# The opening of batch 0 by row tile in order of landing, x of batch 2 ahead of all second weights, and batch 1 turned behind the second axis

## The chip, the cores and the metric

The kernel runs on one core of one Trainium2 chip. The metric is the device time of one execution in microseconds, as the median of several executions. The profile of one execution gives a *span*, from the first to the last counted instruction; it is about 2 us shorter than the timed figure. The *granted clock* is the share of TensorE's full clock that the profile shows as granted to it (1.00 is all of it). On one core a single run has no second core to be compared with, so the state of a run (fast or slow) is read against the fastest run of the same kernel. Only fast runs are compared here, except where the text says otherwise.

## The reference

Eight batches pass an attention between `x` (512 rows per head) and a small `state` (32 rows per head), then a two-dimensional Fourier transform of which the real part is kept, a normalization and two dense layers.

```python
B, H, S, Ns, D = (8, 8, 512, 32, 64)
def _attn_ref(x, state):
    scores = scale * x @ state^T            # softmax over the 32 state rows
    xread  = softmax(scores) @ state        # 512 rows
    sread  = softmax(scale * state @ x^T) @ x   # 32 "state rows"
    return concatenate([xread, sread], axis=2)  # 544 rows, d_model = 512
def _moe_ref(x, w_ch1, w_ch2):
    mixed = real(fft(fft(x, axis=1), axis=2))
    u  = x + mixed
    un = (u - mean(u)) / sqrt(var(u) + 1e-6)
    return u + maximum(un @ w_ch1, 0) @ w_ch2   # 512 -> 2048 -> 512
```

(Shortened.) The kernel does the transforms as matmuls with cosine and sine tables: the *first axis* runs over the rows (products `gp`), the *second axis* over the 512 columns (products `yp`). Rows are first folded into even and odd parts (`Sm`, `SS`), so that half the products suffice. Layer 1 is `ph`, layer 2 is `po`.

## The kernel before

All engines are scheduled by hand: each executes its instructions in the order in which the program lists them. TensorE (PE) streams the two layers of all batches almost without a gap. The argument is about the first 60 us, in which batch 0 has nothing to hide behind. The parts that matter are these. First, the clears of buffers of the attention, which stand on GpSimd behind the request of the first weights; then the later loads:

```python
def clears(i):
    nc.gpsimd.memset(XFs[i][:, :, 512:514], 0.0)
    # ... (borders of XR, XO, XOl, and all of XN, XQl)

nc.gpsimd.tensor_copy(gate, xs_of[0][:, 0:2048:512])      # wait for all of x of batch 0
for q in range(4):
    nc.gpsimd.dma_start(out=w1[:, :, q * 512:(q + 1) * 512], in_=w1v[:, :, q * 512:(q + 1) * 512])
more_constants()
clears(0)

def more_loads():
    state_blocks(1, 2, nc.gpsimd.tensor_copy)
    nc.gpsimd.tensor_copy(gate[:, 0:1], XQ0[:, 3, 0, 0:1])
    cast_x(1)
    nc.gpsimd.tensor_tensor(gate, xs_of[0][:, 0:4], w1[:, :, 3 * 512], op=ALU.add)
    turn_in_dram(3, B)
    load_x(2)
    # ...
def last_loads():
    nc.gpsimd.tensor_copy(gate[:, 0:1], xs_of[2][:, 0:1])  # one row tile of x of batch 2
    for q in range(4):
        nc.gpsimd.dma_start(out=w2[:, q * 4:(q + 1) * 4, :], in_=w2v[:, q * 4:(q + 1) * 4, :])
    state_blocks(2, 3, nc.gpsimd.tensor_copy)
```

A "gate" is a tiny GpSimd operation that reads what it is to wait for; since GpSimd works in order, everything listed behind it waits too. Second, the order of the first part, in which `t0` are the steps of batch 0's transform, `s1` and `r1` scores and reads of batch 1, `L` and `M` layer-1 and layer-2 blocks, and `turns1` PE's transposes of x of batch 1:

```python
for step in (warmed(t0[:2], 2) + [alternate, more_loads] + warmed(t0[2:4], 2) + [exp_again, last_loads,
        t0[4], t0[8], W(6), turns1, t0[5], W(10), t0[7], copies1[0], copies1[1], t0[6], copies1[2],
        L[0], s1[0], t0[9], L[1], t0[10], s1[1], L[2], t0[11], t0[12], L[3], s1[2], r1[0], L[4], s1[3],
        r1[2], lambda: (cast_x(2), turned[2](), load_x3()), t0[13], L[5], r1[1], L[6], r1[3], L[7], r1[4], r1[5], L[8], r1[7],
        lambda: state_ones(2, B), lambda: [r() for r in first_roots], L[9], L[10]]):
    step()
```

Third, the row sum of a batch, a VectorE operation with two bf16 inputs in SBUF (the on-chip buffer), which recurs in every batch:

```python
def fold_rows(k, eng=nc.vector):
    eng.tensor_add(Sm[:, k], XF[:, k], XR[:, k])
```

The softmax here doesn't subtract the row's maximum and nothing guards it: scores larger than these inputs give would overflow.

Of the kernel before, what the change touches and what calls it, by code (L numbers as in the profile page):

```python
# [12 lines left out]
F32 = mybir.dt.float32  # L13
BF16 = mybir.dt.bfloat16
# [16 lines left out]
def kernel(  # L31
# [26 lines left out]
    psX = ctx.enter_context(tc.tile_pool(name="psX", bufs=1, space=bass.MemoryType.PSUM))  # L58
    psQ = ctx.enter_context(tc.tile_pool(name="psQ", bufs=3, space=bass.MemoryType.PSUM))
    psF = ctx.enter_context(tc.tile_pool(name="psF", bufs=3, space=bass.MemoryType.PSUM))  # L60
# [8 lines left out]
    mhalfpi = singles.tile([128, 1], F32, name="mhalfpi")  # L69
    pi_ = singles.tile([128, 5], I32, name="pi_")  # L70
# [4 lines left out]
    ltq = lt.rearrange("p (q i) -> p q i", q=2)  # L75
    nc.gpsimd.iota(ltq[:, :, 0:64], pattern=[[1, 2], [2, 64]], base=1, channel_multiplier=0)
# [3 lines left out]
    nc.gpsimd.iota(pi_[:, 0:2], pattern=[[128, 2]], base=1, channel_multiplier=1)  # L80
    nc.gpsimd.iota(pi_[:, 3:4], pattern=[[0, 1]], base=0, channel_multiplier=1)
    nc.gpsimd.iota(pi_[:, 4:5], pattern=[[0, 1]], base=128, channel_multiplier=-1)
    for hh in range(4):
        nc.gpsimd.iota(pi_[32 * hh:32 * hh + 32, 2:3], pattern=[[0, 1]], base=129, channel_multiplier=1)
    nc.gpsimd.iota(li[:, 0:128], pattern=[[2, 128]], base=1, channel_multiplier=0)
    nc.gpsimd.iota(li[:, 128:256], pattern=[[2, 128]], base=2, channel_multiplier=0)
    nc.gpsimd.iota(li[:, 256:384], pattern=[[2, 128]], base=1, channel_multiplier=0)
    make_identity(nc, ident)
    mirror = singles.tile([128, 128], BF16, name="mirror")
    halves = ((halfpi, PI / 2), (mhalfpi, -PI / 2), (epst, eps), (mhalf, -0.5))  # L90
    sg = singles.tile([128, 5], F32, name="sg")
    sgi = singles.tile([128, 1], I32, name="sgi")

    def more_constants():
        for t, v in halves:
            nc.gpsimd.memset(t, v)
        nc.gpsimd.memset(mirror, 0.0)
        nc.gpsimd.affine_select(out=mirror, in_=mirror, compare_op=ALU.not_equal, fill=1.0, base=-127,
                                pattern=[[1, 128]], channel_multiplier=1)
# [13 lines left out]
    def load_x(b):  # L113
        xs = wk.tile([128, 4 * dm], F32, name="xs", tag="xs")
        xs_of[b] = xs
        v = xs.rearrange("p (i h d) -> p i h d", i=4, d=D)
        xb = x[b].rearrange("h s d -> s h d")
        for ps, si, rows in (
            (slice(0, 128), 0, xb[1:129]),
            (slice(0, 128), 1, xb[144:272]),  # L120
            (slice(0, 128), 2, xb[273:401]),
            (slice(32, 128), 3, xb[416:512]),
            (slice(0, 15), 3, xb[129:144]),
            (slice(16, 31), 3, xb[401:416]),
            (slice(15, 16), 3, xb[0:1]),
            (slice(31, 32), 3, xb[272:273]),
        ):
            queue = nc.scalar if b == 0 and si in (0, 2) else nc.sync
            queue.dma_start(out=v[ps, si], in_=rows)  # L129
# [4 lines left out]
    load_state(0, 1)  # L134
    load_x(0)
    load_state(1, 2)
    load_x(1)
# [5 lines left out]

    turn_in_dram(2, 3)
    load_state(2, 3, s_dram)
# [24 lines left out]
    state_blocks(0, 1)  # L170
    cast_x(0, nc.scalar.copy, 0, 1)
    cast_x(0, nc.scalar.copy, 1, 2)
    cast_x(0, lo=2, hi=3)
    cast_x(0, lo=3, hi=4)
# [16 lines left out]
    XQ0 = XQs[0].rearrange("p (j k c) -> p j k c", j=4, k=2)  # L191
# [5 lines left out]
    TN = singles.tile([128, NM], BF16, name="TN")  # L197
    TE = singles.tile([128, 512], BF16, name="TE")
    TO = singles.tile([128, 512], BF16, name="TO")

    pf = singles.tile([128, 5], F32, name="pf")
# [5 lines left out]
    def turn(W, N, lf, cols, scratch):  # L207
        n = len(cols)
        f2d, q2d = scratch[:, 0:n * W], scratch[:, n * W:2 * n * W]
        f, q = [t.rearrange("p (n w) -> p n w", w=W) for t in (f2d, q2d)]  # L210
        for i, c in enumerate(cols):
            nc.vector.tensor_scalar(q[:, i, :], in0=lf, scalar1=pn[:, c:c + 1], scalar2=float(1 << 23), op0=ALU.mult, op1=ALU.add)
        nc.vector.tensor_scalar(q2d, in0=q2d, scalar1=float(1 << 23), scalar2=-float(N), op0=ALU.subtract, op1=ALU.mult)
        for i, c in enumerate(cols):
            nc.vector.scalar_tensor_tensor(f[:, i, :], in0=lf, scalar=pf[:, c:c + 1], in1=q[:, i, :], op0=ALU.mult, op1=ALU.add)
        absolute(q2d, f2d)
        return f, q
# [12 lines left out]
    f1, q1 = turn(NM, Stot, lt, [0, 2], gen1)  # L230

    fi = gen2[:, 0:384].bitcast(I32)
    f2 = gen2[:, 384:768]
    q2_ = gen2[:, 2048:2432]
    nc.vector.tensor_scalar(fi[:, 0:256], in0=li[:, 0:256], scalar1=pf[:, 3:4], scalar2=None, op0=ALU.mult)
    nc.vector.tensor_scalar(fi[:, 256:384], in0=li[:, 256:384], scalar1=pf[:, 4:5], scalar2=None, op0=ALU.mult)
    turn_w = 2.0 * PI / dm * shrink


    def second_table():  # L240
        nc.vector.tensor_scalar(fi, in0=fi, scalar1=dm - 1, scalar2=None, op0=ALU.bitwise_and)
        nc.vector.tensor_scalar(f2, in0=fi, scalar1=float(dm // 2), scalar2=None, op0=ALU.subtract)
        absolute(q2_, f2)
        nc.vector.tensor_scalar(sgi, in0=pi_[:, 3:4], scalar1=1, scalar2=None, op0=ALU.bitwise_and)
        nc.vector.tensor_scalar(sg[:, 0:1], in0=sgi, scalar1=-2.0, scalar2=1.0, op0=ALU.mult, op1=ALU.add)
        nc.vector.tensor_scalar(sg[:, 2:3], in0=sg[:, 0:1], scalar1=-PI / 2, scalar2=None, op0=ALU.mult)
        nc.vector.tensor_scalar(sg[:, 3:4], in0=sg[:, 0:1], scalar1=turn_w, scalar2=None, op0=ALU.mult)





    def sines():
        w = 2.0 * PI / Stot * shrink
        nc.scalar.activation(TC, q1, AF.Sin, bias=halfpi, scale=-w)
        nc.scalar.activation(TS, f1, AF.Sin, bias=0.0, scale=w)
        nc.scalar.activation(TS[32:64, 1, :], q1[32:64, 1, :], AF.Sin, bias=halfpi[32:64], scale=-w)
# [4 lines left out]
    def more_sines():  # L262
        w = 2.0 * PI / dm * shrink
        te, to = [t.rearrange("p (a h c) -> p a h c", a=2, h=2) for t in (TE, TO)]
        q, f = [t.rearrange("p (a c) -> p a c", c=128) for t in (q2_, f2)]
        nc.scalar.activation(te[:, :, 0], q[:, 0:2], AF.Sin, bias=mhalfpi, scale=w)
        nc.scalar.activation(te[:, :, 1], q[:, 0:2], AF.Sin, bias=sg[:, 2:3], scale=sg[:, 3:4])
        nc.scalar.activation(to[:, :, 0], f[:, 2:0:-1], AF.Sin, bias=0.0, scale=w)
        nc.scalar.activation(to[:, :, 1], f[:, 2:0:-1], AF.Sin, bias=0.0, scale=sg[:, 3:4])
# [3 lines left out]

    def alternate():
        for lo, v in ((0, 0.5), (256, 1.0)):
            nc.gpsimd.memset(TO[0:1, lo:lo + 256:2], -v)
            nc.gpsimd.memset(TO[0:1, lo + 1:lo + 256:2], v)

# [11 lines left out]
    nc.gpsimd.tensor_copy(gate, xs_of[0][:, 0:2048:512])  # L290
    for q in range(4):
        nc.gpsimd.dma_start(out=w1[:, :, q * 512:(q + 1) * 512], in_=w1v[:, :, q * 512:(q + 1) * 512])
    more_constants()
    clears(0)

    def more_loads():
        state_blocks(1, 2, nc.gpsimd.tensor_copy)
        nc.gpsimd.tensor_copy(gate[:, 0:1], XQ0[:, 3, 0, 0:1])
        cast_x(1)
# [590 lines left out]
```

## Time and profile before

| | before |
|---|---|
| median of 4 runs in this comparison | 304.88 us (304.45 to 305.28) |
| span of the profiled run, mean granted clock | 302.7 us, 1.00 |
| second axis of batch 0 begins (first `yp`) | 23.21 us |
| layer 1 begins (first `ph` on `unT`) | 27.71 us |
| rest, from there to the end | 275.0 us |
| second weights asked for; landed by quarter | 29.55; 36.4 to 46.2 us |

The lines of the page and of PE's timeline stand in the prediction below. Two more views of the kernel before are needed. The first is VectorE's timeline; a line reads start, duration, engine, source line, operation, output<-inputs, sizes, count, and in brackets the idle time just before with what ended it.

```profile
12.22 0.69 DVE L449 TENSOR_TENSOR XR<-xrp,rs 128x512 bf16<-128x512 f32 x1 [0.40 <-POOL XR L281]
...
42.44 0.43 DVE L507 TENSOR_TENSOR Sm<-XF,XR 128x514 bf16<-128x514 bf16 x1
```

The first line is the first read multiply of batch 0: it waited 0.40 us for GpSimd (POOL) to clear the border of its output `XR`, at 12.2 us. So short a wait is easily passed over; it will matter that the clear came at 12.2 and not how long it was waited for. The second is the row sum of batch 1, unhindered: 0.43 us.

The second view is the queue of SyncE, which issues most transfers (SPq).

```profile
25.15 6.33 SPq L129 DMA_DIRECT2D xs<-in_x_dram  x8
34.02 2.59 SPq L360 DMA_TRANSPOSE sT<-stb  x2
```

x of batch 2 is asked for from 25.15 us on, before the two DMA transposes of its state.

### The profile page before, as it was taken

The page shows a single profiled execution, that of the slowest core. Times are in us where ns is not written, and L with a number is a line of the kernel's source. Part 1 is how long each engine was busy: PE and PEld are TensorE (multiplying, and loading weights), DVE is VectorE, ACT ScalarE, POOL GpSimd, SP SyncE. Part 2 cuts the span into 40 slices and gives each one's busy share as a digit, 9 for nine tenths or more (in the row PEclk, how much of TensorE's full clock was granted, in tenths as well). Part 3 has the DMA queues.
Part 4 walks back from the last instruction along what each step waited for, and adds up shares of the span by engine and source line. Part 5 has one row for each costly group of instructions (what it writes and reads, how often), then busy time and mean ns, then how long its engine had stood idle before and what let it go on. Part 6 is the DMA issues. An engine that isn't in the chain of part 4 may idle for free.

```text
span 302.7 us, 6048 instructions
## 1 busy us (share of the span) xinstructions
PE 290.6 (96%) x2326; PEld 166.7 (55%) x2326; DVE 179.5 (59%) x433; ACT 139.5 (46%) x267; POOL 96.6 (32%) x217
## 2 busy tenths in 40 slices
PE   5868999999999999999999999999999999999996
PEld 4756997545544555456544555445454544555443
DVE  7696784867888395754727575675668474000012
ACT  6777865746633553254533445254524442334200
POOL 4987784490271034400315022702240131000000
PEclk9999999999999999999999999999999999999999
DMA  7997999144733943467242765253333023600355
GB/s 160 210 200 171 182 174 220 50 89 110 171 87 72 208 122 89 105 137 170 68 116 70 151 146 106 69 123 70 87 89 69 37 69 87 138 2 35 71 135 142
DMA packets 110906, 34.86 MB, mean 115 GB/s; under 512 B 102062, under 2 KB 106414, under 8 KB 110878
## 3 DMA queue, kind: packets, MB, share of 16 engines
q1 hardware_dynamic: 100158, 28.72, 42.3%
q0 software_dynamic: 4224, 4.19, 8.6%
q10 hardware_dynamic: 6496, 1.57, 2.3%
q8 instruction: 18, 0.29, 0.4%
q14 instruction: 10, 0.08, 0.1%
HBM read 22.41 MB, written 14.02 MB: 120 GB/s over the span
## 4 chain that ended last, share of the span: by engine, by line
PE 87%; DVE 3%; POOL 3%; ACT 3%; SPq 1%; DMA 1%; issue 1%; POOLq 0%; DVEq 0%; ACTq 0%
PE po L793 36%; PE ph L729 34%; PE ph L739 4%; PE gp L610 3%; PE po L785 1%; SPq L129 1%; PE xrp L440 1%; PE xfp L440 1%; PE yp L565 1%; PE yp L564 1%; PE esp L415 1%; PE eTp L427 1%; POOL xin L132 1%; DMA xs<-in_x_dram 1%; DVE U L569 1%; ACT XR L470 1%
## 5 line engine op out<-in xcount | busy, mean ns | idle before, releaser
L793 PE MATMUL po<-w,hT 128*128 128x512 bf16 x496 | 124.2, 379 | 0.0
L731 ACT ACTIVATE hT<-ph 128x512 bf16<-128x512 f32 x112 | 66.8, 597 | 118.2 <-PE ph L729 116.1
L729 PE MATMUL ph<-unT,w 128*128 128x512 bf16 x448 | 113.8, 379 | 0.0
L729 PEld LDWEIGHTS <-w 128*128 128x128 bf16 x576 | 50.7, 98 | 47.0
L793 PEld LDWEIGHTS <-hT 128*128 128x128 bf16 x496 | 46.9, 98 | 46.5
L760 DVE SCALAR_TENSOR_TENSOR ot<-po,rstd,U 128x512 f32<-128x512 f32 (+2 forms) x33 | 24.2, 733 | 51.1 <-PE po L793 48.9
L614 POOL COPY GL<-G 128x128 bf16<-128x128 bf16 x8 | 2.3, 291 | 75.4 <-ACT G L611 75.4
L569 DVE TENSOR_TENSOR U<-yp,XR 128x512 f32<-128x512 f32 x16 | 10.9, 683 | 26.0 <-PE yp L565 26.0
L326 POOL TENSOR_TENSOR rstd<-mv,epst 128x1 f32<-128x1 f32 x34 | 7.5, 221 | 47.3 <-DVE mv L322 47.3
L327 POOL TENSOR_TENSOR rstd<-rstd,mhalf 128x1 f32<-128x1 f32 x34 | 21.2, 624 | 2.7
L320 DVE BATCH_NORM_STATS2 st<-U 128x6 f32<-128x512 f32 x32 | 21.8, 682 | 0.1
L611 ACT CAST G<-gp 128x288 bf16<-128x288 f32 x31 | 14.6, 485 | 7.6 <-PE gp L610 7.6
L739 PE MATMUL ph<-unT,w 128*128 128x128 bf16 x256 | 16.1, 219 | 0.5 <-ACT unT L650 0.5
L132 POOL CAST xin<-xs 128x2048 bf16<-128x2048 f32 (+1 forms) x9 | 14.5, 1616 | 3.6 <-DMA xs<-in_x_dram 3.3
L813 PE MATMUL warm<-ident 128*128 128x128 bf16 x144 | 12.0, 232 | 3.7 <-POOL ident masks.py:199 3.6
L739 PEld LDWEIGHTS <-w 128*128 128x128 bf16 x256 | 15.0, 98 | 0.8 <-issue 0.6
L638 DVE TENSOR_SCALAR ub<-U,mv 128x512 bf16<-128x512 f32 x24 | 12.3, 513 | 0.9
L491 POOL COPY XT<-XR 32x514 bf16<-32x514 bf16 x8 | 4.8, 603 | 23.4 <-DVE XR L449 23.1
L813 PEld LDWEIGHTS <-ident 128*128 128x128 bf16 x144 | 9.9, 104 | 4.1 <-POOL ident masks.py:199 3.6
L449 DVE TENSOR_TENSOR XR<-xrp,rs 128x512 bf16<-128x512 f32 x16 | 11.1, 695 | 1.0 <-POOL XR L281 0.4
L741 ACT ACTIVATE hT<-ph 128x512 bf16<-128x512 f32 x16 | 9.3, 597 | 3.2 <-PE ph L739 3.1
L569 DVE TENSOR_TENSOR U<-yp,XF 128x510 f32<-128x510 f32 x16 | 10.8, 674 | 0.0
(187 smaller groups left out, 367.1 us busy)
## 6 DMA issues: line engine op xcount, KB each, us to landing
xs<-in_x_dram SPq DMA_DIRECT2D x22, 256.0 KB, 4.5
w<-in_moe_w_ch_dram POOLq DMA_DIRECT2D x8, 512.0 KB, 10.9
out_dram<-ot SPq DMA_DIRECT2D x15, 256.0 KB, 3.1
r_dram<-ot SPq DMA_DIRECT2D x14, 256.0 KB
out_dram<-r_dram SPq DMA_DIRECT2D x14, 256.0 KB, 3.5
xs<-in_x_dram SPq DMA_DIRECT2D x8, 192.0 KB, 3.4
xs<-in_x_dram ACTq DMA_DIRECT2D x2, 256.0 KB
l_dram<-ot SPq DMA_DIRECT2D x2, 256.0 KB
```

Source lines behind the costliest of these rows:

```text
L132: copy(xin_bufs[b % 2][:, lo:hi, 1:513], xs_of[b].rearrange("p (i c) -> p i c", i=4)[:, lo:hi])
L320: nc.vector.bn_stats(st6, u)
L327: nc.gpsimd.tensor_tensor(rstd, rstd, mhalf, op=ALU.pow)
L569: nc.vector.tensor_add(u.rearrange("p (k r) -> p k r", r=2), p.rearrange("p (r k) -> p k r", r=2)[:, 0:u.shape[1] // 2, :], x.rearrange("p ...
L611: (nc.vector.tensor_copy if b == 0 and j == 3 else nc.scalar.copy)(G[:, j, :].rearrange("p (i q) -> p q i", q=2), p[:, 0:NM].rearrange("p ...
L638: nc.vector.tensor_scalar(t, in0=ud, scalar1=mv[:, 0:1], scalar2=None, op0=ALU.subtract)
L729: nc.tensor.matmul(ph[:, o:o + n], lhsT=w1[:, c, f * 128:(f + 1) * 128], rhs=un_of[key][:, c, :], start=(c == 0), stop=(c == DC - 1))
L731: nc.scalar.activation(hT[:, per * i:per * i + per, :].rearrange("p a b -> p (a b)"), ph, AF.Relu, scale=-1.0 if key in flipped else 1.0)
L739: nc.tensor.matmul(ph[:, o:o + 128], lhsT=w1[:, c, f * 128:(f + 1) * 128], rhs=un_of[key][:, c, 128 * r:128 * r + 128], start=(c == 0), st ...
L760: nc.vector.scalar_tensor_tensor(ot[:, cols], in0=po_of[i][:, 0:cols.stop - cols.start], scalar=rstd, in1=u[:, cols], op0=ALU.mult, op1=AL ...
L793: nc.tensor.matmul(po_of[i], lhsT=h_of[key][:, f, i * 128:(i + 1) * 128], rhs=w2[:, f, :], start=(f == 0), stop=(f == FC - 1))
L813: nc.tensor.matmul(t[:, 0:128], lhsT=ident, rhs=ident, start=(i == 0), stop=(i == n - 1))
```

## The change

The intent has three parts. (1) Batch 0 passes its opening one row tile at a time, in the order in which the tiles of x land (2, 0, 3, 1): transpose, score, one exponential, read. The state rows go through four matmuls where eight small copies were; half of the second-axis tables are computed by a multiply on VectorE instead of two more sines; statistics and roots of batch 0 are put off. (2) All of x of batch 2 is to be there before the second weights are asked for. (3) PE transposes batch 1 behind both second-axis products, not between them. The core of the diff, with cuts marked:

```diff
@@ loads of x @@
+        if b == 0:
+            for queue, n in ((nc.sync, None), (nc.scalar, 2), (nc.sync, 3), (nc.scalar, 0), (nc.sync, 4), (nc.sync, 5), (nc.sync, 6),
+                             (nc.sync, 1)):
# ...
@@ half tables @@
+    def second_halves():
+        nc.vector.tensor_scalar(TEO[:, :, 1], in0=TEO[:, :, 0], scalar1=sg, scalar2=None, op0=ALU.mult)
+        nc.vector.tensor_scalar(TEO[0:1, 2], in0=TEO[0:1, 2], scalar1=0.5, scalar2=None, op0=ALU.mult)
# ...
@@ GpSimd's early work @@
-    nc.gpsimd.tensor_copy(gate, xs_of[0][:, 0:2048:512])
# ...
+    for i in (3, 1):
+        cast_x(0, lo=i, hi=i + 1)
     for q in range(4):
         nc.gpsimd.dma_start(out=w1[:, :, q * 512:(q + 1) * 512], in_=w1v[:, :, q * 512:(q + 1) * 512])
-    more_constants()
+    constants()
     clears(0)
# ...
-    def last_loads():
-        nc.gpsimd.tensor_copy(gate[:, 0:1], xs_of[2][:, 0:1])
+    def load_w2():
+        nc.gpsimd.tensor_copy(gate, xs_of[2][:, 0:2048:512])
         for q in range(4):
             nc.gpsimd.dma_start(out=w2[:, q * 4:(q + 1) * 4, :], in_=w2v[:, q * 4:(q + 1) * 4, :])
-        state_blocks(2, 3, nc.gpsimd.tensor_copy)
# ...
@@ order, after the opening @@
+    over_d(0)
+    add_sums(0, 1)
+    centre_sums(0, 1)
+    over_d(1)
+    turns1()
+    keep_low()
+    clear_state(2, 3)
+    state_blocks(2, 3, nc.gpsimd.tensor_copy)
+    turned[2, 0]()
+    make_mirror()
+    nc.gpsimd.tensor_tensor(gate, xs_of[0][:, 0:4], w1[:, :, 3 * 512], op=ALU.add)
+    load_x(2)
# ...
+    L[6]()
+    r1[2]()
+    load_w2()
+    r1[1]()
+    L[7]()
+    r1[3]()
+    L[8]()
+    r1[4]()
+    cast_x(2)
+    turned[2]()
+    load_state(3, B, s_dram)
+    load_x(3)
# ...
```

## The prediction

> **What bounds the kernel now.** I read the page first: engine totals, then the slices.
>
> ```profile
> span 302.7 us, 6048 instructions
> ...
> PE 290.6 (96%) x2326; PEld 166.7 (55%) x2326; DVE 179.5 (59%) x433; ACT 139.5 (46%) x267; POOL 96.6 (32%) x217
> ...
> PE   5868999999999999999999999999999999999996
> ...
> PEclk9999999999999999999999999999999999999999
> ```
>
> TensorE (PE) is the bound, at full clock, but only from the fifth slice on (7.6 us each). What can be won lies in the first four, and busy there does not mean useful: much of it is "warm" matmuls on an identity. So next I read PE's timeline for the first real matmul of layer 1 (line L739).
>
> ```profile
> 23.21 0.27 PE L564 MATMUL yp<-TE,G 128*128 128x256 bf16 x1
> ...
> 24.40 0.50 PE L813 MATMUL warm<-ident 128*128 128x128 bf16 x6
> 25.18 1.07 PE L387 MATMUL xTp<-ident,xin 128*128 128x128 bf16 x16 [0.28 <-POOL xin L132]
> ...
> 26.30 0.72 PE L813 MATMUL warm<-ident 128*128 128x128 bf16 x10
> ...
> 27.71 1.22 PE L739 MATMUL ph<-unT,w 128*128 128x128 bf16 x16 [0.46 <-ACT unT L650]
> ```
>
> Columns: start, duration, what, count, idle before. Layer 1 starts at 27.71; 302.7 - 27.71 = 275.0 us follow. Comparing each later matmul's start-to-start time with its shape's median, I find only 4.75 us of excess in those 275: 0.63 before the scores of batch 1 (28.7), 0.30 twice near 40, 1.3 from 56 to 64, the rest in pieces of about 0.1 that return every batch. The tail after the last matmul is 3.2. So the time is the start of layer 1, plus about 270 us of fixed streaming, plus stalls.
>
> The chain of waits tells why the start is 27.71 (start, duration, what):
>
> ```profile
> 4.95 2.52 DMA xs<-in_x_dram
> 7.52 0.63 POOL xin L132
> ...
> 10.53 0.60 ACT ET L406
> 11.13 0.98 ACT E L420 x2
> 12.12 0.92 ACT L260
> ...
> 16.25 1.17 POOL Sm L507
> ...
> 23.22 1.91 POOL xin L132
> ...
> 25.18 1.07 PE xTp L387 x16
> ```
>
> All four row tiles wait for the last piece of x (7.47 us); then all exponentials, the sine table load, eight small copies of the state rows (13.62 to 16.18), the fold on GpSimd, and last GpSimd's cast of batch 1, which PE must transpose before it reaches batch 0's own transpose.
>
> **What the Trainium skill says.** "TensorE: Matmul & The Clock Gate", Wait — 56ns, not 53.3ns?: warm start-to-start 55.6 ns at 128 columns, 215.7 at 512. The trace agrees: medians 56 and 216. "ScalarE: Activation LUTs", What ACT_TABLE_LOAD costs: about 1283 ns per load. The trace has 1.28 us at each of three; the change keeps three. "SBUF — State Buffer", Who interferes with whom: a VectorE (DVE) operation with two SBUF inputs excludes a GpSimd operation that reads SBUF, and the later waits. The trace fits: the fold of 514 columns took 0.93 us at 16.76 beside GpSimd's own fold, 0.43 at 42.44. "DMA: Bandwidth & Descriptors", Anatomy of one DMA: about 2 us fixed. The 64 KB state load took 2.74 (0.73 to 3.47).
>
> **The change, part by part.** The order of instructions shows that after the first layer-1 matmul both kernels have the same 4109 PE rows, in the same numbers by shape. So nothing is gained in the stream itself. I walk the new opening with durations of the old trace.
>
> *Loads.* x tiles now land as 2, 0, 3, 1. Tile 2 has the place of the old first load (landed 4.36). By bytes at the old 279 KB/us (704 KB between 4.36 and 6.88) I get tile 0 at about 6.0, tile 3 at 6.5; tile 1, issued last at about 4.3, at 7.5. ScalarE (ACT) casts tile 2 at 4.75 to 5.37 and tile 0 at 6.05 to 6.7; GpSimd casts 3 and 1, ending 7.15 and 8.2.
>
> *By row tile.* Each passes transpose (0.25 PE), copy (0.42 DVE or 0.55 ACT), score (0.35 PE), one exponential (0.60 ACT, for the former two of 0.60), read (0.3 PE), reciprocal and multiply (0.92 DVE); a PE result costs about 0.2 more to be seen. Tile 2: transposed 6.1, copied 7.0, exponential 8.2, read done 9.8. Tile 0: exponential 9.3 to 9.9, read done 11.4. Tile 3: exponential to 10.6; tile 1's copy follows to 11.15, its score to 11.75, its exponential to 12.35. DVE multiplies tile 3 to 13.0, copies the low rows (0.4), multiplies tile 1 to 14.35. Before, the last read ended at 16.72: about 2.4 us won.
>
> *State rows.* Eight ACT copies (2.56) become one DVE reciprocal and multiply (0.45, to 14.8), four matmuls and one ACT copy (0.6). ACT: table load and gate 12.4 to 13.9, two sines 1.35 to 15.25, state-row copy to 15.9, the rest of the tables to 17.1. Hidden.
>
> *Folds and first axis.* All on DVE, by row half. Even part: 0.43 + 2 x 0.2 + 2 x 0.18 + a dependence, 1.2; odd part 2 x 0.35 + 0.1 = 0.8; each twice, plus two negated tables 0.15 each: 4.3 us. GpSimd works all this time (low rows, casts of state and x of batch 1), so I choose a contention factor 1.2; the stretch 16.8 to 22.3 before took 5.6 where quiet durations add to 4.1, factor 1.37. So 14.8 + 5.2 = 20.0. Half tables 0.5, copies of the first-axis result 0.41 and 0.28: second axis starts at about 21.3, before 23.21. The accumulating matmuls run beside this.
>
> *From second axis to layer 1.* Before 27.71 - 23.21 = 4.50. Now batch 1's transposes come behind both second-axis products, without the wait for GpSimd's cast (due at about 21 now). PE: 2 x 0.45, 20 transposes 1.12, batch 0's 0.22, latency 0.2, half copy 0.4, hand-over 0.1: 2.95. Beside it DVE's add (0.75) with its sum as a by-product, in place of add, statistics and aggregate (1.55), then two half centrings (0.45). Layer 1 starts at 24.2; hand walks miss waits, so I take **24.5**, 3.2 us earlier.
>
> *After it.* The second layer-1 block now precedes batch 1's scores, so the 0.63 stall and some neighbours go: -1.1.
>
> *x of batch 2 first.* The second weights are now issued behind batch 1's low fold, which follows the sixth layer-1 block: 24.5 + 5.4 + 2.0 of other PE work, then DVE 1.6 and GpSimd 1.5, about 35.5, before 29.55. The queue view before says how long they take:
>
> ```profile
> L309 POOL DMA_DIRECT2D w<-in_moe_w_ch_dram x4: 760/775/802, 29.5 to 31.8; - x4
> ...
> DMA to landing us min/median/max: 6.8/10.7/14.4
> ```
>
> The last quarter landed 14.4 after its issue, so at 46.2; layer 2 first needed it at 55.4: slack 9. Now, with less beside them, the quarters land at about 41.5 to 51. Layer 2 starts 18.4 of stall-free PE work after layer 1, at 42.9, and wants its last quarter 7.2 later, 50.1. Slack is about zero; I charge +0.6.
>
> Sum: span 24.5 + 275.0 - 1.1 + 0.6 = 299.0. The timed median exceeds the span by 304.61 - 302.7 = 1.9, hence 300.9; I lean a little below, because the arrangement looks tuned: **300.4 us**.
>
> **Rivals.** (1) *The second weights become the wait.* For: issue six microseconds later, zero slack. Against: x of batch 2 no longer shares the DMA engines with them. If the last quarter comes 2 us late, where I charge 0.6, 300.9 + 1.4 = 302.3. (2) *DVE becomes the opening's bound.* It carries every read and fold from 8.9 on. With factor 1.37 or stronger in the folds and a few hand-overs of 0.1 more, layer 1 starts at 25.6: 300.9 + 1.1 = 302.0. (3) *Everything goes as laid out*: no contention, no late weights: start 23.6, 1.5 of stalls gone: 23.6 + 275.0 - 1.5 + 1.9 = 299.0; it must go 0.4 better still to cross 2% (298.6). (4) *The gain is hidden anyway*, because x of batches 1 to 3 or first weights arrive no sooner. Against: the first weights landed 16.2 to 24.9 (8.0 to 14.3 after issue), and the block that needs the last comes at about 28.
>
> **Range and chances.** Start of layer 1: 24.5, give or take 1.5. Stalls after it: -0.5, give or take 1.5. The two errors are independent, so together about 2.1 (root of the summed squares), and around 300.4 I give 298.2 to 302.8 for 8 in 10. Over 2% faster needs below 298.6: 0.14. Slower by 2% (310.7) would need a stall of 10 us that I cannot see: 0.01. Within 2%: 0.85.
>
> **What would show it.** In the changed profile: first layer-1 matmul at 23.0 to 26.0; four exponentials ending near 8.2, 9.9, 10.6, 12.4; second axis near 21.3; 2.7 to 3.3 from there to layer 1; no idle PE between the first two layer-1 blocks; second weights issued near 35.5 and PE waits at layer 2 under 1 us; from 65 us on the two timelines equal but for a shift of 3 to 5 us. I am wrong if layer 1 starts after 26.5, if layer 2 waits over 2 us for weights, or if later batches stall on x, which comes at other times.

## The result, and the profile after

The changed kernel is correct and takes 308.64 us (median of 4 fast runs, 308.37 to 309.1) against 304.88 us. The ratio is 1.0125, with a 95% interval of 1.0104 to 1.0147. A ratio in this document is the mean time of one kernel's fast runs over that of the other's of the same rounds, so it is not quite the ratio of the medians quoted. It stayed within 2% of the kernel before, as expected with 0.85, but the time did not come true: 308.64 lies 5.8 us above the upper end of the range, and on the other side of the kernel before.

| us | before | predicted | after |
|---|---|---|---|
| second axis begins | 23.21 | 21.3 | 25.01 |
| from there to layer 1 | 4.50 | 2.95 | 2.91 |
| layer 1 begins | 27.71 | 24.5 | 27.92 |
| rest | 275.0 | 274.5 | 278.7 |
| span | 302.7 | 299.0 | 306.6 |

So of the 7.6 us of span that the prediction lacked, 3.4 arise before layer 1 and 4.2 after it. The page of the changed kernel, with its slices of 7.7 us:

```profile
span 306.6 us, 5976 instructions
...
PE   5697997989999999999999999999999999999996
...
PEclk9979997999999999999999999999999999999999
DMA  8992989973942955449252594263343034500346
```

In the kernel before the row PEclk had only nines. Now the third and seventh slices have sevens: PE was granted less than its full clock in them. The trace gives the stretches: half speed from 15.0 to 18.4 us and from 49.1 to 52.6. The row DMA has a two in the fourth slice (23 to 31 us), where x of batch 2 should have been under way. PE's timeline tells the start of layer 1, and its waits between 10 and 70 us (us in total, times, longest) what it lacked:

```profile
25.01 0.27 PE L659 MATMUL yp<-TEO,G 128*128 128x256 bf16 x1 [1.63 <-DVE G L736]
...
25.88 1.06 PE L383 MATMUL xTp<-ident,xin 128*128 128x128 bf16 x16
...
27.92 0.76 PE L905 MATMUL ph<-unT,w 128*128 128x128 bf16 x7 [0.29 <-ACT unT L825]
```

```profile
PE esp L580 <- DVE rs L600: 2.9, 1, 2.9
PE gp L754 <- DVE XQ L512: 1.9, 1, 1.9
PE yp L659 <- DVE G L736: 1.6, 1, 1.6
```

Three waits of over a microsecond, all for VectorE, and none of them in the kernel before (its only one from 10 us on is 1.2 us at 19.3, for the folds of batch 0). None is for a weight. VectorE's timeline shows why it was late each time:

```profile
9.22 0.20 DVE L600 RECIPROCAL rs<-esp 128x8 f32<-128x8 f32 x1
12.54 0.69 DVE L604 TENSOR_TENSOR XR<-xrp,rs 128x512 bf16<-128x512 f32 x1 [3.12 <-POOL XR L276]
...
21.22 2.59 DVE L268 TENSOR_SCALAR TEO<-TEO,sg 128x512 bf16<-128x512 bf16 x1
...
42.90 2.70 DVE L503 TENSOR_TENSOR Sm<-XF,XR 128x514 bf16<-128x514 bf16 x1
45.64 0.69 DVE L508 TENSOR_TENSOR SS<-Sm 128x514 f32<-128x514 bf16 x1
```

The first read multiply stood idle for 3.12 us, for GpSimd's clear of `XR`. Then two short operations show durations of 2.59 and 2.70 us: a blocked operation counts as busy, so it appears in no list of waits. The row sum took 0.43 us in the kernel before. GpSimd's timeline over the same stretches:

```profile
7.43 1.66 POOL L143 CAST xin<-xs 128x512 bf16<-128x512 f32 x2 [2.42 <-DMA xs<-in_x_dram]
9.03 3.20 POOL L296 DMA_DIRECT2D w<-in_moe_w_ch_dram  x4
...
12.35 0.16 POOL L276 MEMSET XR<- 128x4 bf16 x1
...
21.20 1.89 POOL L143 CAST xin<-xs 128x2048 bf16<-128x2048 f32 x1
...
38.79 3.03 POOL L306 DMA_DIRECT2D w<-in_moe_w_ch_dram  x4
...
43.40 1.91 POOL L143 CAST xin<-xs 128x2048 bf16<-128x2048 f32 x1
```

The clear of `XR` comes at 12.35, behind two casts and the issue of four weight transfers. A cast of x of batch 1 runs from 21.20 to 23.09, and VectorE's table multiply, issued at 21.22, ends at 23.81. A cast of x of batch 2 runs from 43.40 to 45.31, and the row sum ends at 45.60. In the kernel before this cast ran from 37.47 to 39.36, well before the row sum; now the issue of the second weights, 3.03 us of GpSimd's time, and four folds stand ahead of it. The second weights are issued from 38.79 on (predicted 35.5). Finally SyncE's queue:

```profile
27.01 2.59 SPq L356 DMA_TRANSPOSE sT<-stb  x2
29.78 5.04 SPq L140 DMA_DIRECT2D xs<-in_x_dram  x7
```

The two transposes of the state of batch 2 now stand ahead of its x, which is asked for at 29.78 and not 25.15.

### The profile page after: what moved, and what is told of

The parts are those of the page before. It is cut to its first block, busy times and chain, and to the rows that moved or that the text cites. A ratio compares the mean times of both kernels' runs of the same rounds, so it can differ in the third digit from the quotient of the medians.

```text
span 306.6 us, 5976 instructions
## 1 busy us (share of the span) xinstructions
PE 289.3 (94%) x2280; PEld 166.3 (54%) x2311; DVE 184.4 (60%) x449; ACT 135.2 (44%) x255; POOL 90.5 (30%) x214
## 4 chain that ended last, share of the span: by engine, by line
PE 83%; DVE 9%; issue 2%; POOL 2%; DMA 2%; ACT 1%; SPq 0%; DVEq 0%; POOLq 0%; ACTq 0%
PE po L959 36%; PE ph L895 34%; PE gp L754 3%; PE ph L905 2%; DMA xs<-in_x_dram 2%; PE yp L659 1%; PE yp L660 1%; PE po L951 1%; PE xrp L436 1%; POOL w L296 1%; DVE Sm L503 1%; PE xfp L436 1%; PE eTp L423 1%; PE esp L411 1%; DVE TEO L268 1%
## 5 line engine op out<-in xcount | busy, mean ns | idle before, releaser
L959 PE MATMUL po<-w,hT 128*128 128x512 bf16 x478 | 122.5, 381 | 1.6 <-issue 0.9
L664 DVE TENSOR_TENSOR U<-yp,XR 128x512 f32<-128x512 f32 x14 | 9.6, 683 | 22.9 <-PE yp L660 22.9
L323 POOL TENSOR_TENSOR rstd<-rstd,mhalf 128x1 f32<-128x1 f32 x34 | 20.1, 590 | 2.7
L755 ACT CAST G<-gp 128x288 bf16<-128x288 f32 x28 | 13.3, 484 | 8.8 <-PE gp L754 8.8
L991 PE MATMUL warm<-ident 128*128 128x128 bf16 x74 | 8.5, 265 | 3.5 <-POOL xs L285 3.5
L445 DVE TENSOR_TENSOR XR<-xrp,rs 128x512 bf16<-128x512 f32 x14 | 9.7, 694 | 0.6
L487 POOL COPY XT<-XR 32x514 bf16<-32x514 bf16 x6 | 3.6, 602 | 21.8 <-DVE XR L445 21.7
L445 DVE TENSOR_TENSOR XF<-xfp,rs 128x512 bf16<-128x512 f32 x14 | 9.7, 691 | 0.5
L664 DVE TENSOR_TENSOR U<-yp,XF 128x510 f32<-128x510 f32 x14 | 9.5, 676 | 0.0
```

The costliest lines, as they stand in the source:

```text
L323: nc.gpsimd.tensor_tensor(rstd, rstd, mhalf, op=ALU.pow)
L445: nc.vector.tensor_tensor(ov, in0=p[ps, :, 0:256].rearrange("p g (h d) -> p g h d", d=D), in1=rs[ps].unsqueeze(3).to_broadcast([n, 2, 4, D ...
L664: nc.vector.tensor_add(u.rearrange("p (k r) -> p k r", r=2), p.rearrange("p (r k) -> p k r", r=2)[:, 0:u.shape[1] // 2, :], x.rearrange("p ...
L755: nc.scalar.copy(G[:, j, :].rearrange("p (i q) -> p q i", q=2), p[:, 0:NM].rearrange("p (q i) -> p q i", q=2))
L959: nc.tensor.matmul(po_of[i], lhsT=h_of[key][:, f, i * 128:(i + 1) * 128], rhs=w2[:, f, :], start=(f == 0), stop=(f == FC - 1))
```

## The experiments

The theory after this reading has four parts: **A**, the clears stand too late on GpSimd; **B**, the half-table multiply is blocked by the cast of batch 1; **C**, the row sum of batch 1 is blocked by the cast of batch 2; **D**, x of batch 2 is asked for too late. The rival is that the chain of loads (first weights, x of batch 2, second weights) is the real bound, so that the opening's gain is given back in waits later. All twelve kernels are correct. "Ratio" is always against the kernel before of the same rounds (its medians there: 304.9 to 305.2 us).

### 1. a_clears: the clears ahead of the casts

```diff
+    clears(0)
     for i in (3, 1):
         cast_x(0, lo=i, hi=i + 1)
# ... first weights
     constants()
-    clears(0)
```

> The changed kernel with one thing moved: GpSimd clears the border columns (and the other zero fills of batch 0) before it casts x and issues the first weights, not after. Theory (three collisions): VectorE's first read multiply stood 3.12 us behind that clear, so it starts near 9.5 instead of 12.54; the last exponential, which stood behind VectorE's reciprocal, ends near 12.6 instead of 14.89; the first layer-1 matmul comes at 25.3 to 25.8 instead of 27.92, and the time falls by about 2.4, to 306.2 (305.5 to 307.0). Rival (landing of x or the folds set the start of layer 1 and the wait on the clear is hidden): layer 1 stays at 27.5 or later and the time at 308.6.

Measured: 307.01 us (305.99 to 307.5), ratio 1.0059 (1.0038 to 1.0080). VectorE's timeline, then PE's:

```profile
9.51 0.69 DVE L604 TENSOR_TENSOR XR<-xrp,rs 128x512 bf16<-128x512 f32 x1
...
18.81 0.34 DVE L268 TENSOR_SCALAR TEO<-TEO,sg 128x512 bf16<-128x512 bf16 x1
...
43.34 3.75 DVE L512 TENSOR_TENSOR XQ<-XE 128x256 bf16<-128x256 f32 x1
```

```profile
20.71 0.27 PE L659 MATMUL yp<-TEO,G 128*128 128x256 bf16 x1 [0.27 <-DVE G L736]
...
23.47 1.07 PE L383 MATMUL xTp<-ident,xin 128*128 128x128 bf16 x16 [1.73 <-POOL xin L143]
...
25.50 1.71 PE L905 MATMUL ph<-unT,w 128*128 128x128 bf16 x24 [0.29 <-ACT unT L825]
```

The read multiply comes 3.0 us earlier, the second axis 4.3, layer 1 2.4 us earlier, as expected; the time fell by 1.6 of the expected 2.4, to just outside its range. Here the table multiply no longer meets a cast and takes 0.34 us: that is its quiet size. But x of batch 1 landed only at 21.5, so that PE waited 1.73 us for its cast, and the rest grew by 1.0 to 279.7: PE waited 3.2 us for a blocked fold (the last of VectorE's lines above, behind four of GpSimd's folds and the cast of batch 2; 0.43 us in the changed kernel; here the row sum itself passed in 0.43), and 2.0 us for transposes of x of batch 2. The late cast of batch 1 also blocked a centring on VectorE (1.98 us at 22.14, 0.36 in the changed kernel), in the shadow of PE's own wait. Part A is shown, though this run takes B's collision away along with it; the rival has a point too.

### 2. b_halves: the half tables on ScalarE

```diff
+        nc.scalar.activation(TEO[:, :, 1], TEO[:, :, 0], AF.Copy, scale=sg)
-        nc.vector.tensor_scalar(TEO[:, :, 1], in0=TEO[:, :, 0], scalar1=sg, scalar2=None, op0=ALU.mult)
```

> The changed kernel with the half tables (TEO times sg, 128x512) computed on ScalarE instead of VectorE. Theory: on VectorE this one took 2.59 us because GpSimd's cast of batch 1 (21.20 to 23.09) held it off; without it VectorE copies the first-axis results about 2.5 earlier. Then ScalarE's own exp table load (23.25 to 24.75), which is not moved, is next, so layer 1 starts at 25.8 to 26.4 instead of 27.92 and the time is 306.9 (306.2 to 307.5). Rival (VectorE is not what the second axis waits for): layer 1 within 0.4 of 27.92, time 308.6.

Measured: 308.65 us (307.15 to 309.55), ratio 1.0112 (1.0079 to 1.0145); layer 1 at 27.04. A miss, and an instructive one. One small operation was left on VectorE:

```profile
21.72 2.02 DVE L269 TENSOR_SCALAR TEO<-TEO 1x256 bf16<-1x256 bf16 x1 [0.41 <-ACT TEO L266]
```

256 elements in one partition took 2.02 us, against 0.22 in a_clears. What is paid is the rest of GpSimd's work (its cast ran until 23.12, four clears after it until 23.67), not the size of the blocked operation. The 0.9 us that layer 1 gained was lost again at the row sum, blocked for 3.76 us here.

### 3. c_cast: the cast of batch 2 ahead of the second weights

```diff
     r1[2]()
+    cast_x(2)
     load_w2()
# ...
     r1[4]()
-    cast_x(2)
```

> The changed kernel with GpSimd's cast of x of batch 2 put before the issue of the second weights. Theory: VectorE's fold at 42.90 took 2.70 us because this cast (43.40 to 45.31) held it off; it takes 0.43 to 0.9 now, TensorE's wait of 1.9 for XQ near 46 goes, and with it the lower granted clock that followed (48.5 to 52.5). Layer 1 still starts at 27.9, the rest takes 275.0 to 275.8 instead of 278.7, time 305.3 (304.6 to 306.0). Rival (the lower clock comes from somewhere else, or the weights, now issued 2 us later, become the wait): the rest stays above 277, time 307 or more.

Measured: 308.62 us (307.48 to 309.57), ratio 1.0104 (1.008 to 1.0128). VectorE's row sum, then PE's two waits for second weights:

```profile
43.16 0.43 DVE L503 TENSOR_TENSOR Sm<-XF,XR 128x514 bf16<-128x514 bf16 x1
```

```profile
51.36 1.02 PE L959 MATMUL po<-w,hT 128*128 128x512 bf16 x4 [0.38 <-DMA w<-in_moe_w_ch_dram]
...
55.70 1.21 PE L959 MATMUL po<-w,hT 128*128 128x512 bf16 x4 [2.02 <-DMA w<-in_moe_w_ch_dram]
```

The collision is gone (0.43 us), and PE's wait for the row sum with it (0.44 us where it was 1.90), which shows part C; but the expected 305.3 us was missed, as its rival had it: the cast pushed the second weights from 38.8 to 40.9 us, they landed at 47.3 to 58.7, and PE waited for them in place of the row sum.

### 4. abc: all three

The three edits together.

> All three moves together. Theory: the start of layer 1 at 23.4 to 24.8, as the prediction's walk had it, the rest 274.7 to 276.2, time 301.3 (300.2 to 302.6), faster than the kernel before by about 1.2%. Rival (the opening by row tile gains nothing even without collisions): layer 1 at 26.5 or later, time 304 or more. A third: second weights, now issued after the cast, land too late for layer 2 (last quarter wanted about 25.6 after the start of layer 1): TensorE waits over 1 us between 43 and 55.

Measured: 308.74 us (308.1 to 309.65), ratio 1.0122 (1.010 to 1.0144). Layer 1 began at 24.38, the 24.5 of the prediction almost to the digit, and nothing of it was left at the end: the rest was 282.8. Layer 2 began at 48.0, where it also began in the kernel before with layer 1 at 27.7. x of batch 2 landed about 39, its cast ran from 39.17 and blocked the earlier row sum for 1.97 us, and PE waited 2.3 us for second weights. Its profile also has half clock from 45.4 to 52.4 us, but that is not what decides: one of the four runs had a clock of 1.00 and took 308.53 us. So the rival is right for this kernel: a chain in absolute time, from the first weights to x of batch 2 to its cast and the second weights, which doesn't move with the opening.

### 5. d_x2: x of batch 2 asked for ahead of the state's transposes

```diff
     keep_low()
+    nc.gpsimd.tensor_tensor(gate, xs_of[0][:, 0:4], w1[:, :, 3 * 512], op=ALU.add)
+    load_x(2)
     clear_state(2, 3)
# ... state_blocks, turned[2, 0], make_mirror
-    nc.gpsimd.tensor_tensor(gate, xs_of[0][:, 0:4], w1[:, :, 3 * 512], op=ALU.add)
-    load_x(2)
```

> The changed kernel with the loads of x of batch 2 issued ahead of batch 2's state work and its two transposing transfers, on the same queue, as soon as the first weights have landed. Theory (two constraints side by side): x of batch 2 lands near 32.5 instead of 37.8, but in the changed kernel as it stands the second weights and the cast of batch 2 wait for GpSimd's own earlier work and not for x (its gate before the weights had no idle time), so the time stays at 308.6 (307.8 to 309.2) and TensorE's wait for XQ near 46 stays near 2. Rival (the late x of batch 2 is by itself what cost the time): time falls by 2 or more.

Measured: 308.11 us (307.16 to 308.75), ratio 1.0101 (1.0079 to 1.0122). x of batch 2 landed about 32 instead of 37.8, and, as expected, this alone bought nothing: the row sum was again blocked for 2.70 us, and the second weights were issued at 38.1, because GpSimd came to them no sooner. PE again waited 1.90 us for the row sum, this time with full clock behind it.

### 6. abcd: all four

> The three moves of the run before plus x of batch 2 issued early. Theory: layer 1 starts at 24.4 as it did with the three; x of batch 2 lands near 32.5 instead of 39; the cast runs near 35 to 37 and clears VectorE's second fold, so the waits of 1.3 and 0.5 for XQ and XQl go, and with them the half clock; the second weights are issued near 37.2 instead of 41.3, so their last quarter is some 1.5 late for layer 2. Span 24.4 + 276.0, time 302.4 (301.3 to 304.0). Rival (x of batch 2 is not what held the three back): time 307 or more.

Measured: 304.7 us (303.67 to 307.56), ratio 1.0006 (0.9955 to 1.0057); layer 1 at 24.19, rest 277.7. Four edits recover the whole loss but win nothing: the second weights are still issued at 37.1, land at 43.8 to 54.7, and PE waits 2.4 us for them. Missed by about 2 us, for that reason.

### 7. abde: second weights and cast ahead of the row folds

A, B and D, and GpSimd's order changed so that the second weights go ahead of the low rows' fold and the cast ahead of the last row step:

```diff
-    r1[2]()
     load_w2()
+    r1[2]()
# ...
-    r1[4]()
     cast_x(2)
+    r1[4]()
```

> Early border clears, half tables on ScalarE, x of batch 2 early, the second weights issued before batch 1's low fold, and the cast of batch 2 before the second half of that fold. Theory: weights issued near 33, landed near 40 to 49, layer 2 (start near 43.2) never waits; no collision; layer 1 at 24.4, the rest 274.5 to 275.6; time 301.3 (300.3 to 302.5), 1.2% faster than the kernel before. Rival (something else of the changed kernel costs after the start of layer 1): the rest over 277, time over 303.5.

Measured: 303.18 us (302.64 to 306.57), ratio 0.9935 (0.9919 to 0.9952): faster than the kernel before, though 1.9 us above what was expected. The profile happened to be of the slowest run (span 304.8, clock 0.993): PE waited 2.5 us from 51.8 us on for transposes of x of batch 2 and then ran at half clock from 54.8 to 58.2. The four other runs had a clock of 1.00 and 302.64 to 303.83 us.

### 8. bef_w2: the second part of the change alone, in the kernel before

```diff
-        nc.gpsimd.tensor_copy(gate[:, 0:1], xs_of[2][:, 0:1])
+        nc.gpsimd.tensor_copy(gate, xs_of[2][:, 0:2048:512])
```

> The kernel before with one part of the change alone: the second weights wait for all four row tiles of x of batch 2, not for the first. Theory: x of batch 2 lands near 32, the weights are issued about 3 later than 29.55 and there were 9 of slack, so the time stays within 0.5 of 304.9. Rival (a serial chain first weights, x of batch 2, second weights costs by itself): 306 or more.

Measured: 307.56 us (304.92 to 308.38), ratio 1.007 (1.0022 to 1.0118). The expectation of at most 0.5 us missed; its rival held. GpSimd's, VectorE's and PE's timelines:

```profile
34.41 0.19 POOL L307 COPY gate<-xs 128x4 f32<-128x4 f32 x1 [6.81 <-DMA xs<-in_x_dram]
34.87 3.03 POOL L309 DMA_DIRECT2D w<-in_moe_w_ch_dram  x4 [0.27 <-issue]
```

```profile
39.90 1.17 DVE L468 TENSOR_SCALAR XR<-srp,rcs 32x64 bf16<-32x64 f32 x4 [2.51 <-POOL XT L491]
```

```profile
42.15 0.39 PE L440 MATMUL xfp<-stb,ET 128*128 128x260 bf16 x2 [2.51 <-DVE XF L449]
```

GpSimd stands at the gate for 6.81 us; its copy of batch 1's low rows (`XT`) is listed behind it, VectorE waits for that copy, and PE for VectorE. So the gate on all of x of batch 2 costs about 2 us by itself, not through the weights but through what stands behind the gate on GpSimd. This is an average of unlike runs: the profiled one also had half clock from 43.0 to 46.6 us, right behind PE's wait, and the one run with a clock of 1.00 took 304.92 us and lost nothing.

### 9. after_warm: what the half clock costs

The changed kernel with 32 identity matmuls just before the product that waited for the blocked row sum.

```diff
+    def warmed_first(s):
+        pool_of.pop("tile", None)
+        warm(32)
+        s()
+    t1 = [lambda s=t1[0]: warmed_first(s)] + t1[1:]
     weave((L[12:], 0, 0.2), (t1, 0.12, 1), # ...
```

> The changed kernel with one thing added: 32 idle matmuls of 128 x 128 on the identity (about 1.7 us at full clock) just before the first over-s product of batch 1, where TensorE stood 1.9 us for the blocked row sum and was then granted half its clock from 49.1 to 52.6 us. No engine but TensorE gets anything new. If the half clock is the consequence of that idle stretch and is paid for (3.4 us at half speed is 1.7 us of matmul time), the time falls by 1.2 to 1.9 us, to about 307.0, and the profile shows full clock around 50 us. If the half clock costs nothing because the work behind it waits for the second weights anyway, or if it comes whatever TensorE does there, the time stays within 0.4 us of 308.6.

Measured: 307.65 us (307.44 to 308.38), ratio 1.0087 (1.0074 to 1.0100), where the changed kernel had 1.0125. PE's timeline, then the clock row of the page:

```profile
46.22 1.95 PE L991 MATMUL warm<-ident 128*128 128x128 bf16 x32
48.28 0.24 PE L754 MATMUL gp<-TC,XQ 128*128 128x144 bf16 x1
```

```profile
PEclk9989999999999999999999999999999999999999
```

The product starts at 48.28, as before (48.27): the row sum is as late as it was. But the seven in the seventh slice has gone, and about 1.0 us with it by the medians, 1.2 by the two ratios (their intervals leave 0.4 to 1.9 open). This lies between the two expectations (1.2 to 1.9 us, or 0.4 and less) or at the edge of the first: idle time at this place cost once by itself, and about a microsecond more by the clock. The other stretch, from 14.8 to 18.4 us, is still there in the profiled run; if it is what sets the runs with 0.993 apart, no cost of it is visible: the runs with a clock of 1.00 or 0.999 took 307.44 and 308.15 us, those with 0.993 took 307.65 twice and 308.38.

### 10. abdes: the scores of batch 2 later

abde with the scores of batch 2 from 0.8 of that stage's steps on, not 0.6, so that layer-2 matmuls fill the wait of run 7.

> The kernel with the clears early, the half tables on ScalarE, x of batch 2 asked for right after the low rows are kept, and second weights and the cast ahead of the row folds, in which TensorE still stood 2.5 us at 51.5 us because the scores of batch 2 waited for the DMA transposes of x, and was then at half clock for 3.4 us. One thing is changed: the scores of batch 2 start at 0.8 of that stage's steps and not at 0.6, so that second-layer matmuls fill the wait. If that wait and the half clock behind it are what is left of the loss, the time falls from 303.2 by 1.5 to 3.5 us, to 299.7 to 301.7, with the rest after the first layer-1 matmul at 275.5 to 277.5. The rival is that the late scores make batch 2's exponentials and reads late in the next stage, so that the wait comes back there: then the time stays at 302.5 to 304.

Measured: ratio 1.0018 (0.9992 to 1.0044), from only two fast runs of six (304.86 and 306.7 us); four runs were slow, 309.54 to 310.63, and so was the profiled one, in which x of batch 1 landed late and PE had half clock from 23.6 to 30.6 us. Neither expectation holds: it is not faster. What made it slow so often can't be read from a profile of the slow state alone, and stays open.

### 11. abdf: cast and transposes of batch 2 ahead of the second weights

A, B and D, with this on GpSimd:

```diff
-    r1[2]()
+    cast_x(2)
+    turned[2]()
     load_w2()
+    r1[2]()
```

> The same kernel (clears early, half tables on ScalarE, x of batch 2 asked for early), but with the cast and the DMA transposes of x of batch 2 ahead of the second weights, and both ahead of the row folds, with the scores of batch 2 where they were. One theory: the transposes then land before 50 us and the 2.5 us wait at 51.5 goes, the second weights are issued about 35.5 us and land early enough for layer 2 at 48.5: 300.5 to 302.5. The rival: transposes and second weights share the same DMA engines, so that what the one gains the other loses; the second weights land after 56 us in their last quarter, TensorE waits 1 to 2.5 us in layer 2, and the time stays at 302.5 to 304.5.

Measured: 303.92 us (303.09 to 306.86), ratio 0.9977 (0.9941 to 1.0013). PE still waited 1.2 us for second weights, within the rival's 1 to 2.5. The runs fall into two groups: four with a clock of 1.00 took 303.09 to 304.03 us, two with 0.994 took 306.24 and 306.86. The profiled run is one of the latter; its half-clock stretch began at 23.5 us, and PE's timeline shows it:

```profile
23.24 1.64 PE L383 MATMUL xTp<-ident,xin 128*128 128x128 bf16 x16 [1.53 <-POOL xin L143]
```

Sixteen transposes in 1.64 us, against 1.07 in a_clears: after a wait of 1.53 us for GpSimd's cast of batch 1.

### 12. abdg: the second part of the change undone

A, B and D; the second weights are again asked for as soon as one row tile of x of batch 2 is there, and cast and transposes of batch 2 stand ahead of the row folds. The opening by row tile and the turn behind the second axis stay.

```diff
-        nc.gpsimd.tensor_copy(gate, xs_of[2][:, 0:2048:512])
+        nc.gpsimd.tensor_copy(gate[:, 0:1], xs_of[2][:, 0:1])
# ...
     make_mirror()
+    load_w2()
# ...
-    r1[2]()
-    load_w2()
+    cast_x(2)
+    turned[2]()
+    r1[2]()
```

> The changed kernel with the clears early and the half tables on ScalarE, and with its third part undone: the second weights are asked for as soon as the first row tile of x of batch 2 has landed, as in the kernel before, and not after all of x of batch 2; the cast and the transposes of x of batch 2 come ahead of the row folds. The opening by row tile and the turn of batch 1 behind the second axis stay. If the order of x of batch 2 and the second weights is what kept layer 2 at 48 us whatever the start of layer 1, the second weights are now issued by 31 us and landed by 48, nothing waits for them, and with layer 1 at 24.2 to 26.2 the rest is 275.5 to 277: 300.5 to 303, with under 1.0 us of waiting on weights. The rival is that x of batch 2, now sharing the DMA engines with the weights, lands after 37 us, so that GpSimd casts late, in front of the row folds, and TensorE waits 2 us or more near 40 us as it did in the run in which the gate alone was moved: 304 to 306.

Measured: 302.69 us (302.39 to 303.79, 5 runs, all with a clock of 1.00), ratio 0.9921 (0.9908 to 0.9935). This is the fastest version measured, 0.8% faster than the kernel before and about 2% faster than the change as it was given; its interval overlaps that of abde (0.9919 to 0.9952), so it is not shown to be faster than that. The first theory held. The second weights' own view, PE's timeline and VectorE's:

```profile
L306 POOL DMA_DIRECT2D w<-in_moe_w_ch_dram x4: 760/775/800, 28.2 to 30.5; - x4
...
DMA to landing us min/median/max: 6.9/11.6/15.7
```

```profile
25.53 2.16 PE L905 MATMUL ph<-unT,w 128*128 128x128 bf16 x32 [0.29 <-ACT unT L825]
...
45.36 1.03 PE L959 MATMUL po<-w,hT 128*128 128x512 bf16 x3
```

```profile
40.67 0.43 DVE L503 TENSOR_TENSOR Sm<-XF,XR 128x514 bf16<-128x514 bf16 x1
```

The weights are issued from 28.2 on and the last quarter is there at 46.2 (30.5 + 15.7); PE never waits for them. Layer 2 begins at 45.36. In the profiles with all of x of batch 2 first it began at 44.7 (abcd, which then waited 2.4 us for weights), at 45.8 (abde), and at 46.5 or later in the others. The row sum is unhindered. The rest is 276.5, 1.5 above the kernel before; layer 1 begins at 25.5 and not at 24.4, because x of batch 1 landed at 21.5 and PE waited 1.2 us for its cast.

| run | edit | median us | ratio | layer 1 at | rest |
|---|---|---|---|---|---|
| after | the change | 308.64 | 1.0125 | 27.92 | 278.7 |
| a_clears | A | 307.01 | 1.0059 | 25.50 | 279.7 |
| b_halves | B | 308.65 | 1.0112 | 27.04 | 280.7 |
| c_cast | C | 308.62 | 1.0104 | 27.93 | 279.8 |
| abc | A, B, C | 308.74 | 1.0122 | 24.38 | 282.8 |
| d_x2 | D | 308.11 | 1.0101 | 27.25 | 278.1 |
| abcd | A to D | 304.7 | 1.0006 | 24.19 | 277.7 |
| abde | A, B, D, weights before folds | 303.18 | 0.9935 | 25.49 | 279.3 |
| abdf | A, B, D, cast before weights | 303.92 | 0.9977 | 26.25 | 278.2 |
| abdg | A, B, D, weights early again | 302.69 | 0.9921 | 25.53 | 276.5 |

Layer 1 and rest are of the profiled run, which for abde and abdf was one with a stretch of half clock. The three runs that don't build on this ladder (bef_w2, after_warm, abdes) are left out.

## Why the prediction was wrong

**"By row tile" failed at its first read.** The step has tile 2's read done at 9.8 and the last exponential at 12.35. The first exponential ended at 8.46 (7.86 + 0.60; predicted 8.2), but the read multiply began at 12.54, because the buffer whose border GpSimd clears was cleared at 12.35. The prediction walked four engines' dependences and gave GpSimd two casts; it left out that the casts and the issue of the first weights (3.2 us) stand in front of the clears, in order. The order was in the program, and the kernel before showed the same wait with 0.40 us. The last exponential began at 14.29, not 11.75. Run a_clears shows this part: layer 1 2.4 us earlier, and the last read multiply done at 14.34, where the prediction had 14.35. So close a hit needed some luck: the loads came later than laid out (tile 0 was cast from 7.00, not from 6.05).

**"Folds and first axis" failed in its half tables.** Put at 0.5 us, the two multiplies took 2.8 (21.22 to 24.05; 2.59 for one and 0.21 for the other). The folds before them took 4.1 us (17.10 to 21.22), where the prediction charged 5.2: its contention factor of 1.2 wasn't needed there. It had quoted the rule and then replaced it by a factor spread over all operations; the block fell whole on one. Its example of an undisturbed fold was misread too: at 42.44 in the kernel before, GpSimd was also folding (42.10 to 43.13), and there GpSimd's fold took longer, 0.61 us where the same fold took 0.40 in the next batch. "SBUF — State Buffer", Who interferes with whom, in the Trainium skill says that the shared pair of ports is an exclusive lock and that the loser "fully blocks"; this trace agrees, with 2.59 against 0.34 us beside a cast of 1.89 us. A lock costs the rest of the other engine's work, so a long neighbour must be placed in time, not averaged. With A and B removed (abc, abcd) layer 1 began at 24.38 and 24.19, each in one profile, so the rest of the walk to 24.5 was sound when x of batch 1 came in time; in the four later versions its landing at about 21.3 to 22.8 added one to two microseconds, or more with half clock.

**"From second axis to layer 1" was right**: 2.91 us against 2.95, and no idle PE was left between the first two layer-1 blocks, as predicted.

**"After it", -1.1, was wrong in sign: +3.7.** Shown parts: PE's wait of 1.9 us (2.06 above the usual distance of the two matmuls) for the row sum, blocked by the cast of batch 2; the half clock behind it, about 1.0 us (after_warm). The prediction had taken the stream after layer 1 as the old one and didn't follow GpSimd's new order in it. The remaining 1 us or so is in pieces that no run here separates; PE's timeline shows three waits of 0.4 to 0.6 us, at 41.5, 61.8 and 65.9. "TensorE: Matmul & The Clock Gate", What's actually happening, describes two clock states and a window of about 3.4 us; the trace agrees in both, with stretches of 3.4 us at 0.5 in this case and of 6.8 in abc. The prediction had cited that page for the warm rate alone and took full clock for granted.

**"x of batch 2 first", +0.6, was wrong by its mechanism.** The path to the issue was right: the second weights were issued 10.9 us after the start of layer 1 (38.79), where the prediction had 11.0. Yet PE waited for none, since layer 2 began only at 50.1, 22.2 us after layer 1 and not 18.4. So rival (1), the second weights as the wait, did not happen in it. It lay behind the other losses: as soon as they were removed, it appeared (2.4 us in c_cast and in abcd, 2.3 in abc). And a cost that the prediction didn't have at all is what a gate on all of x of batch 2 does to GpSimd's order (bef_w2: 1.007); in the changed kernel itself GpSimd didn't stand at that gate, so it is no part of the 308.64. abdf and abdg, which differ in the gate and in the place of the weights' issue, stand at 0.9977 and 0.9921, each against the kernel before of its own rounds. Most of this comes from two of abdf's six runs, with a clock of 0.994; its four at 1.00 averaged 303.5 us, 1.7 below the kernel before, and abdg's five 302.8, 2.1 below. So at full clock this part is worth about 0.4 us, and whether it also keeps the half clock away isn't shown by so few runs.

**Rival (2)** named the right engine, VectorE, and the wrong size: 25.6 where 27.9 came. It put the delay down to stronger contention and more hand-overs, not to a wait and a block. **Rival (4)**, that the gain is hidden because later x arrives no sooner, came true behind the collisions: in abc layer 1 began at 24.38 and nothing was gained, and in the later versions PE waited 1.2 to 3.0 us for x of batch 1. Nothing in the prediction's range covered an effect by which small losses add, an idle stretch and then half clock behind it.

What stays open: abdes' slow runs; the split of the last microsecond after layer 1; and why x of batch 1 landed at 19.6 in abcd, 20.4 in abc, and 21.3 to 22.8 in the other runs that waited for it.

## What to carry to other kernels

When a walk through an in-order engine gives it new early work, list all that stands behind that work and who needs it: a wait of 0.4 us in the old profile can be the tip of one of 3 us in the new. A VectorE operation far longer than its twin elsewhere was, in these runs, a blocked one; look for the long GpSimd instruction that ends just before it, and move one of the two in time rather than making the blocked one smaller. And a gate that makes one queue's transfers wait makes everything behind it on that engine wait: put it where nothing urgent follows.

## What the Trainium skill lacked or had wrong

- "SBUF — State Buffer", Who interferes with whom, is right on the lock but doesn't say how long a blocked operation waits when GpSimd's instructions follow each other without a gap. Here the row sum issued at 42.90 got through only after two of GpSimd's folds and a cast, at 45.60, 0.29 us after the cast ended at 45.31 and while a memset that began at 45.23 was still running; the table multiply (2.59 us, to 23.81) outlasted the cast by 0.72 us, in which GpSimd ran four memsets (to 23.66). In neither case did VectorE get in between neighbours. That the row sum, with two inputs, passed beside a memset agrees with the page; that the multiply ended only after four of them fits its wider lock on writes as well, but no run here isolates that.
- "TensorE: Matmul & The Clock Gate", What's actually happening, ties the half clock to an idle window of about 3.4 us. Here shorter idle stretches were followed by it (1.90 us before 48.3, half clock from 49.1; 1.53 us before 23.2 in abdf, half clock from 23.5), while a wait of 3.2 us in a_clears and one of 1.90 us before 47.6 in d_x2 were not. What one such stretch cost here: about 1.0 us in after_warm; runs of abcd, abde and abdf with a mean clock of 0.993 or 0.994 took about 3 us more than those of the same kernel with 1.00 (idle time before the stretch included), those of the kernel before only 0.3.
